# Two engines share the statistics at a stage's end: an interleaved FFT-filter and S4 kernel on one Trainium2 core

## The chip, the cores and the metric

The kernel runs on one core of one Trainium2 chip. The core has four compute engines with a queue of instructions each: TensorE (PE, matrix products; its weight loads are shown apart as PEld), VectorE (DVE), ScalarE (ACT) and GpSimd (POOL). A fifth queue, SyncE (SP), issues most DMA transfers. Each engine works its queue strictly in order, and semaphores hold an instruction until what it needs is done. Matrix products land in PSUM, which the kernel hands out as eight banks of 128 partitions by 512 fp32 numbers; all else is in SBUF. The metric is the device time of one execution in microseconds, the median of several.

## The reference

Two layers, applied in turn and twice (A, B, A, B), on `x` of 2048 positions by 512 channels in fp32:

```python
def _A_ref(x, w_r, w_i):                       # spectral filter (GFNet)
    X = rfft2(x); X = X * (w_r + 1j * w_i)
    return irfft2(X, s=(S, D))
def _B_ref(u, ...):                            # S4 long convolution
    dt = exp(log_dt)[:, None]
    P = exp((dt * A)[:, :, None] * l)          # A = A_re + 1j A_im, l = 0..2047
    K = einsum("dn,dnl,dn->dl", Cc, P, dt * Bc).real
    y = irfft(rfft(pad(u)) * rfft(pad(K)))[:L] # along the positions, 2L long
    return y + u * Dskip
x = x + _A_ref(_layernorm(x), A_w_r, A_w_i)
x = x + _B_ref(_layernorm(x), ...)             # and both once more
```

`_layernorm` takes mean and variance over the 512 channels of a position, with 1e-5 added to the variance. K does not depend on `x`, so its spectrum is computed once.

## The kernel before, in words

**Tiling.** `x` stays in SBUF as 16 "lines" of 128 positions by 512 channels, four to a "group". Both transforms are matrix products with cosine and sine tables, split into factors. Work is cut into pieces, each a small generator that says on which engine its next step runs and what it waits for.

**Stages.** Four stages follow each other: stage 0 (K's spectrum and layer A's first pass, with the norms for layer B), stage 1 (layer B's first pass, called B0 below), stage 2 (layer A's second pass, A2), stage 3 (layer B's second pass, B1). For each, a planner (`Clock`) simulates engines, banks and buffers with fixed costs, and at every moment emits, of the pieces that are ready, the one with the best rank. The ranks are the table `ORDER`: per kind of piece a number for each piece and a shift for each of its steps. What the planner emits is final: it is the order of each engine's queue on the chip, whatever the real times.

**End of A2.** `inv_a(1, s2)` runs once per line: four matmuls L890 into one bank; ScalarE copies it out, L894 and L895; POOL folds it, L901 to L903; one matmul L907; VectorE adds that to the line in three instructions, L911 to L913, and takes its statistics, `moments`, L591 (bn_stats) and L592 (bn_aggr). After each fourth line `spread` has ScalarE take the square root of the group's variances (L625) and VectorE the reciprocal (L627) and the bias −mean × reciprocal (L629). `norm_b` then writes the normed line into `xn`, the upper half of the tile Y, on ScalarE (L639, Identity with a scale and a bias per position).

**Layer B.** `forward_b(r, i)` makes product i of 16: two matmuls (L951; four rows of the profile) into a pair of PSUM banks, over 32 channels of all 16 lines, and therefore after all 16 norms; VectorE transposes the pair into P (L955), which frees the banks. `step_b` makes 16 spectra from these, multiplies them with K's (L963 matmuls, L985 copy of K, L996 on VectorE, L999 and L1003 beside it) and starts the inverse (L1011, copied out by L1018). `turn_b` transposes again (L1034), `inv_b` makes the last matmuls (L1050, L1055), and `close_b` sends the result out. In stage 1 the last pieces of K's spectrum still run at the start: copy L1291, matmul L1309, transpose L1313 and store L1316.

In the working part a row's name tells a tile: `ps` is a PSUM bank, `wk` a working buffer, `x` the lines, `Y` and `Ya` the two large tiles, `mv`, `rs` and `nb` the mean and variance, the reciprocal and the bias of a group.

Of the kernel before, what the change touches and what calls it, by code (L numbers as in the profile page):

```python
# [40 lines left out]
    (0.050611, {"load_in": ([-48.73, -49.67, -13.2, 200.39, 38.48], [21.36, 0]),  # L41
             "load_n": ([170.88], [17.74, 32.32, 39.11, 0]),
             "load_ra": ([122.74], [-34.24, -26.17, 0]),
             "load_h": ([189.13], [-1.1, 0]),
             "load_da": ([87.12], [11.37, 0]),
             "load_rb": ([156.61], [-6.7, 0]),
             "polar_k": ([188.86], [0, 0, -10.23, 4.9, 30.71, 8.86, -8.44, 0]),
             "octant_k": ([195.76], [0, 0, 30.82, 0]),
             "log_k": ([198.17], [7.12, -1.53, 0]),
             "phase_k": ([54.98], [9.47, -22.65, -34.9, -26.84, -10.4, 0]),  # L50
             "parts": ([-1.02, 52.39, 180.27], [-16.65, -3.98, -14.47, -25.06, -3.65, 0]),
             "load_k": ([0.46, 24.35, 26.66, 90.14, 113.68, 14.97, 134.95, 135.35], [-10.85, -5.26, 0]),
             "exp_k": ([31.12, 30.01, 26.72, -30.41, 4.2, 26.79, 11.64, 78.24, -6.3, 0.57, 130.4, 110.04, 7.61, 12.56, -2.93, 102.4, -2.77, 13.49, 75.18, 23.12, 30.66, 48.47, 2.53, 144.61, -3.85, 206.61, 15.72, 29.43, 103.43, 4.73, 22.38, 4.74, 79.71, 78.57, 136.47, 110.99, 104.63, 0.06, 9.23, -3.76, 152.2, 80.58, 107.2, 21.85, 20.82, 98.84, 202.47, 24.5], [-0.87, -2.09, 0]),
             "unit_k": ([-5.49, 9.8, -46.86, 52.48, -7.95, 46.43, 63.91, 65.15, -59.42, -20.7, 96.11, -25.05, -14.14, 82.98, 95.72, 99.58, 47.51, 48.51, 62.41, 78.63, 79.81, 82.78, 85.31, 89.29, 89.73, 95.21, -3.54, 105.55, 118.51, 120.91, 137.32, 137.55], [34.37, 31.83, 13.78, 42.41, 30.07, 30.15, 32.23, 39.12, 35.89, 0]),
             "rows_k": ([48.24, 146.28, 190.46, 133.31, 5.29, 9.15, 119.72, 143.74], [-28.96, -21.87, -21.87, -15.39, -19.71, -19.24, 0]),
             "sums": ([68.3, 174.15, 8.23, 16.19], [32.48, 30.78, 32.04, 16.99, 13.91, 7.66, 34.05, -0.27, 37.66, 2.46, 0]),
             "spread": ([17.55, 129.21, 18.82, 50.21, 18.68, 37.9, 26.12, 42.83, 81.35], [-14.02, -12.43, 0]),
             "moments": ([48.6, 168.25, 167.06, 170.68], [-35.07, 0]),
             "forward_a": ([237.18, 160.57, 32, 190.87, 212.59, 50.71, -0.81, 157.11, 67.95, -12.81, 211.5, 73.12, 9.09, 134.47, 112.18, 101.62], [-41.16, -32.05, -34.91, -48.86, -16.07, 0]),
             "first_a": ([-4.49, -18.8, 15.57, 3.63, 80.21, 17.42, 26.99, 60.31, 117.89, 120.37, 101.06, 141.83, 161.84, 119.48, 213.35, 138.85], [-2.64, 38.82, -12.59, 0.61, 1.12, 22.42, 1.12, 9.82, -0.59, 0.31, 31.16, 0]),  # L60
             "inv_a": ([119.1, 153.39, 154.78, -12.8, 176.52, 180.93, 165.04, 176.64, 179.21, 212.81, 173.77, 172.16, 165.73, 204.44, 203.24, 205.17], [6.59, 5.52, -33.78, -0.86, 39.16, 4.18, 0]),
             "norm_b": ([134.64, -13.39, 180.42, -19.04, 155.44, 123.24, 118.52, -19.66, -9.73, 62, -15.3, 11.32, -33.63, 181.42, 143.72, 95.73], [3.13, 0]),
             "tables": ([52.58], [-16.4, 0])}),
    (0.106371, {"forward_b": ([29.41, 45.28, 85.57, 67.58, 7.03, 50.48, 14.98, 21.28, 109.8, 98.41, 90.83, 85.95, 131.45, 144.47, 19.4, 145.79], [-5.6, -0.98, 0]),
             "step_b": ([7.93, 28.66, 33.01, 13.11, 38.16, 40.28, 33.13, 39.52, 42.94, 57.01, 56.63, 59.65, 66.64, 96.31, 104.01, 83.04], [-17.85, -14.85, -17.85, -16.95, -25.44, -25.72, -28.7, 4.97, -22.24, -44.63, 0]),
             "turn_b": ([44.83, 28.62, 85.03, 95.07, 45.09, 44.66, 52.6, 91.28, 99.52, 44.73, -14.85, 63.29], [3.25, 0]),
             "inv_b": ([119.63, 32.94, 28.08, 78.54, 29.81, 90.22, 22.29, 1.94, 55.77, 84.98, 61.47, 22.25, 20.09, 22.33, 52.81, 56.82], [-14.24, 9.33, 0]),
             "close_b": ([57.52, 57.61, 79.73, 44.41, 4.32, 13.02, 36.04, 99.27], [-0.22, 0]),
             "spread": ([3.27, -6.17, -43.17, -3.6], [44.68, 11.41, 0]),
             "forward_a": ([98.41, 41.14, 22.14, 43, 25.09, 29.39, 49.01, 44.67, 27.43, 43.03, 112.28, 138.34, 59.73, -4.87, 70.46, 89.13], [-11.44, 15.32, -1.65, 0, 11.1, 0])}),  # L70
    (0.010000, {"load_du": ([164.21], [-44.93, 0]),
             "first_a": ([179.48], [-24.75, -4.44, -14.35, 0, 72.12, 2.11, 1.29, 6.33, 6.76, 0.12, 14.34, 0]),
             "group_a": ([194.01, 232.24, 217.79, 202.63, 238.5, 131.16, 205.2, 199.29, 233.37, 217.41, 208.36, 198.07, 122.44, 202.74, 207.67], [-103.75, -39.32, -54.25, -22.22, -23.2, -100.35, -23.93, -3.71, -36.68, -38.02, -25.08, -23.93, 0]),
             "inv_a": ([180.35, 141.51, 145.93, 197.94, 183.36, 101.66, 176.36, 118.03, 147.61, 232.02, 160.93, 213.63, 186.51, 139.07, 199.6, 146.8], [55.08, 1.48, -4.95, -5.13, 25.36, -6.18, -13.95, 0]),
             "spread": ([177.02, 157.89, 140.63, 190.66], [0, -2.36, 0]),
             "norm_b": ([139.04, 206.02, 221.71, 116.37, 218.26, 121.3, 209.11, 190.78, 125.49, 189.55, 217.69, 200.09, 212.22, 217.5, 116.15, 186.47], [-0.59, 0])}),
    (0.191249, {"forward_b": ([16.74, -30.74, 7.86, -14.65, -23.43, -19.05, -24.28, -7.05, 54.87, 33.03, -16.53, 38.87, 21.87, -22.87, 3.42, -24.9], [-14.33, 68.5, 0]),
             "step_b": ([-48.3, -52.59, -66.06, -59.51, -63.91, -44.14, -38.35, -44.74, -47.06, -34.23, -22.73, -28.22, -1.93, -46.76, 16.96, 16.68], [16.57, 35.26, 26.88, 18.48, 44.4, 11.44, 27.32, 94.94, 0]),
             "turn_b": ([-14.27, -34.14, 44.25, 43.22, 23.59, 43.79, -0.43, 14.42, -40.01, 29.56, 38.77, 2.4], [13.89, 0]),
             "inv_b": ([20.94, 61.81, 32.87, 19.49, -33.55, 25.49, 9.2, -18.63, 60.91, -35.33, 1.86, -32.68, 12.23, 21.87, 69.24, 30.39], [76.77, -10.14, 0]),  # L80
             "close_b": ([-46.35, -28.26, 12.32, -60.23, -24.23, 4.46, -64.62, -57.64], [30.99, 0])}),
# [403 lines left out]
class Net:  # L485
# [134 lines left out]
    def spread(self, i, st, act=False, part=slice(0, 4)):  # L620
# [4 lines left out]
        self.nc.scalar.activation(rs, mv[:, :, 1], AF.Sqrt, bias=self.eps)  # L625
        yield "DVE"
        self.nc.vector.reciprocal(rs, rs)  # L627
        if act:
            self.nc.vector.scalar_tensor_tensor(b, mv[:, :, 0], -1.0, rs, op0=OP.mult, op1=OP.mult)  # L629
# [308 lines left out]
    def norm_b(self, r, s2, st):  # L938

        yield "ACT", self.after((id(st), s2)), self.emitted(("group", 1), 16) if r else self.emitted("product", 32)  # L940
        self.norm(s2, st, True, self.xn[r][:, s2, :])
        self.mark("norm_b", r)

    def forward_b(self, r, i):

        nc = self.nc
        yield "PE p:u", self.after(("norm_b", r), 16)
        p = self.psum("u")
        for h in range(2):
# [1 line left out]
            nc.tensor.matmul(p[:, 512 * h:512 * h + 512], self.Rb[o, :], self.xn[r][o, :, 32 * i:32 * i + 32], start=True, stop=True)  # L951
# [561 lines left out]
```

## Time and profile before

| | |
|---|---|
| median of 3 runs | 712.26 us (711.82 to 712.85) |
| profiled execution | 709.7 us, span 707.9 us |
| mean granted TensorE clock | 0.927 |
| PE busy | 580.8 us (82% of the span) |
| DVE busy | 546.8 us (77%) |
| ACT busy | 425.8 us (60%) |
| POOL busy | 314.9 us (44%) |
| share of the chain of waits | PE 12%, DVE 9%, ACT 2% of the span among the largest groups |

The span runs from the first to the last instruction; the execution's time holds 1.8 us more around it. No engine is busy throughout, so the shares say little: what counts is, at each place, which wait ends last. The views that tell this are the chain of waits (what the last instruction waited for, followed back), the busy time by stretches of the span, and the timeline of one engine. In a timeline a row gives start, length, engine, line, operation, tile, and in brackets the idle time before it with what ended it.

### The profile page before, as it was taken

How to read it: one execution, taken by the hardware profiler on the slowest of the kernel's cores; microseconds unless marked ns; L12 is line 12 of the kernel's file. 1: busy time of each engine (PE TensorE's matmuls, PEld its weight loads, DVE VectorE, ACT ScalarE, POOL GpSimd, SP SyncE). 2: the span in 40 equal slices, each digit the busy share in tenths (PEclk: the TensorE clock that was granted, in tenths of full speed). 3: DMA queues.
4: the chain of work that ended last, by engine and by line, in shares of the span. 5: the costliest groups of instructions: out<-in, count | busy, mean ns of one | idle time of the engine just before them, and what ended most of it. 6: DMA issues, size and time to landing. Idle time of an engine off the chain costs nothing. (4 is left out here: it accounts for less than half of the span.)

```text
span 707.9 us, 19921 instructions
## 1 busy us (share of the span) xinstructions
PE 580.8 (82%) x8424; PEld 372.5 (53%) x8424; DVE 546.8 (77%) x807; ACT 425.8 (60%) x742; POOL 314.9 (44%) x299
## 2 busy tenths in 40 slices
PE   0768988989979999796689998579999981789965
PEld 0767866557544444344236564178778750246621
DVE  1697738787697999988694698876988596984994
ACT  6898369898878969787426553067564436035510
POOL 0652108477294462646024562076665670057710
PEclk9969989999999999887699999779999995999996
DMA  8707443221106520101575876260564013025376
GB/s 211 213 16 239 155 130 96 83 74 53 61 25 193 172 75 2 60 4 62 200 274 186 267 243 191 62 262 1 188 228 146 1 44 134 1 92 170 120 213 189
DMA packets 45857, 90.92 MB, mean 128 GB/s; under 512 B 3944, under 2 KB 25960, under 8 KB 44744
## 3 DMA queue, kind: packets, MB, share of 16 engines
q1 hardware_dynamic: 35016, 77.07, 34.4%
q10 hardware_dynamic: 10752, 12.58, 5.0%
q8 instruction: 66, 1.08, 0.6%
q14 instruction: 23, 0.19, 0.1%
HBM read 62.51 MB, written 27.13 MB: 127 GB/s over the span
## 5 line engine op out<-in xcount | busy, mean ns | idle before, releaser
L1003 POOL TENSOR_TENSOR wk<-wk 128x1024 f32<-128x1024 f32 x32 | 75.9, 2380 | 122.7 <-ACT wk L999 122.7
L1269 POOL TENSOR_TENSOR Y<-wk,Y 128x1024 f32<-128x1024 f32 x32 | 76.7, 2396 | 56.2 <-issue 27.6
L1011 PE MATMUL ps<-wk 32*64 32x256 f32 x2048 | 69.7, 381 | 2.5 <-DVE wk L996 0.9
L951 PE MATMUL ps<-Y,cRb 64*128 64x512 f32 x128 | 37.4, 698 | 29.3 <-ACT Y L639 21.7
L1011 PEld LDWEIGHTS ps<-wk 32*64 32x64 f32 x2048 | 47.1, 131 | 26.0 <-issue 7.7
L996 DVE TENSOR_TENSOR wk<-ps,wk 128x1024 f32<-128x1024 f32 x32 | 38.9, 1220 | 24.9 <-PE ps L963 20.3
L1247 DVE SCALAR_TENSOR_TENSOR wk<-wk,ps 128x1024 f32<-128x1024 f32 x32 | 38.9, 1214 | 22.7 <-ACT wk L1245 22.5
L1282 PE MATMUL ps<-Y 128*32 128x64 f32 x2048 | 39.4, 234 | 14.6 <-POOL Y L1270 11.8
L1231 ACT ACTIVATE Y<-ps 128x1024 f32<-128x1024 f32 x48 | 47.7, 1033 | 4.8 <-PE ps L1215 4.5
L1282 PEld LDWEIGHTS ps<-Y 128*32 128x32 f32 x2048 | 34.2, 119 | 29.9 <-POOL Y L1270 21.1
L1215 PE MATMUL ps<-wk,Y 96*128 96x512 bf16 x128 | 40.6, 394 | 8.4 <-ACT Y L1231 4.8
L1050 PE MATMUL ps<-Y,cRbT 128*64 128x512 f32 x128 | 34.5, 692 | 13.9 <-DMA Y<-yi 7.2
L1270 POOL TENSOR_TENSOR Y<-wk,Y 128x512 f32<-128x512 f32 x32 | 43.6, 1363 | 0.0
L999 ACT COPY wk<-ps 128x512 f32<-128x512 f32 x32 | 18.8, 587 | 41.3 <-PE ps L963 35.0
L1263 DVE TENSOR_TENSOR Y<-ps,Y 128x1024 f32<-128x1024 f32 x32 | 38.8, 1213 | 3.2 <-PE ps L1282 2.1
L827 POOL TENSOR_TENSOR x<-x 128x257 f32<-128x257 f32 x16 | 11.6, 723 | 64.4 <-PE ps L850 35.6
L1034 DVE STREAM_TRANSPOSE Y<-Y 128x1024 f32<-128x1024 f32 x16 | 36.7, 2315 | 4.3 <-ACT Y L1018 4.3
L951 PEld LDWEIGHTS ps<-Y,cRb 64*128 64x128 f32 x128 | 12.3, 213 | 52.6 <-ACT Y L639 24.1
L1245 ACT ACTIVATE wk<-ps,magic 128x1024 f32<-128x1024 f32 x32 | 35.5, 1120 | 6.2 <-PE ps L1215 5.9
L1252 ACT ACTIVATE ps<-wk 128x1024 f32<-128x1024 f32 x32 | 32.8, 1026 | 6.3 <-DVE wk L1247 2.4
L1255 ACT ACTIVATE wk<-wk,quarter 128x1024 f32<-128x1024 f32 x32 | 36.4, 1137 | 0.1
L907 PE MATMUL ps<-wk,cRaT 128*128 128x512 f32 x64 | 34.3, 629 | 2.1 <-ACT wk L882 1.9
(232 smaller groups left out, 1631.2 us busy)
## 6 DMA issues: line engine op xcount, KB each, us to landing
yk<-wk SPq DMA_DIRECT2D x8, 1024.0 KB
wk<-yk SPq DMA_DIRECT2D x16, 512.0 KB
khat<-wk ACTq DMA_DIRECT2D x16, 512.0 KB
wk<-khat SPq DMA_DIRECT2D x16, 512.0 KB
Y<-in_W_dram SPq DMA_DIRECT2D x12, 515.0 KB
x<-in_cPa_dram SPq DMA_DIRECT2D x16, 384.0 KB
Y<-in_cGa_dram SPq DMA_DIRECT2D x12, 384.0 KB
x<-in_W_dram SPq DMA_DIRECT2D x16, 258.0 KB
```

What stands on the lines that cost most here:

```text
L951: nc.tensor.matmul(p[:, 512 * h:512 * h + 512], self.Rb[o, :], self.xn[r][o, :, 32 * i:32 * i + 32], start=True, stop=True)
L996: nc.vector.tensor_tensor(t0, X[:, 0, :, None, :].to_broadcast(four), kh[:, 0, None, :, :].to_broadcast(four), op=OP.mult)
L1003: nc.gpsimd.tensor_tensor(t1, xi[:, :, None, :].to_broadcast(four), kh[:, 1, None, :, :].to_broadcast(four), op=OP.mult)
L1011: nc.tensor.matmul(v[i // 2][64 * a:64 * a + 64, 512 * (i % 2):512 * (i % 2) + 256], self.Ib[o, g, a, b, :], t[o, x, k, :], start=n == 0, ...
L1034: self.nc.vector.transpose(y.rearrange("p s d -> p d s"), self.P[r][e][:, :, o:o + 32].rearrange("p k d -> p d k"))
L1215: self.nc.tensor.matmul(p, f[:, c:c + 128], self.oh[:k, o:o + 512], start=True, stop=True)
L1231: nc.scalar.activation(m[:, :, 1024:] if i == 2 else m[:, i, :1024], p.rearrange("p (i m) -> p i m", i=2) if i == 2 else p, AF.Exp)
L1247: nc.vector.scalar_tensor_tensor(s, c, MAGIC, p, op0=OP.subtract, op1=OP.subtract)
L1263: nc.vector.tensor_tensor(E[:, 1, :1024], p, m[:, :1024], op=OP.mult)
L1269: nc.gpsimd.tensor_tensor(E[:, 0, :1024], c, m[:, :1024], op=OP.mult)
L1270: nc.gpsimd.tensor_tensor(rows(E[:, 0, 1024:]), back(c[:, 512:]), rows(m[:, 1024:]), op=OP.mult)
L1282: nc.tensor.matmul(pk[32 * j:32 * j + 32, 64 * e:64 * e + 64], E1[:, r, i, :], E2[:, r, i], start=r == 0, stop=r == 1)
```

## The change

**Statistics on ScalarE.** For groups 0 and 1 of A2's inverse (eight lines, `SQUARED`) `moments` is replaced by two passes of ScalarE over the line: Identity with scale −1/512 and an accumulator, which leaves minus the mean; then Square with that as bias and an accumulator, which leaves 512 times the variance. What the passes write goes into the line's place in `xn`, where the norm overwrites it. The square root of these groups takes the scale 1/512, and the bias's sign is turned.

**Norms on VectorE.** Lines 8 and 9 (group 2) are normed by VectorE (`norm`'s other branch, subtract and multiply) in both passes.

**Products in parts.** Products 4 and 6 of the first pass and 1 and 15 of the second (`FIRST`) are issued in two steps: the columns of groups 0, 1 and 3 when these are normed, and group 2's columns when it is.

**The planner.** ScalarE's passes over SBUF in stages 2 and 3 cost 0.17 more in its own reckoning, and all numbers of `ORDER` are new.

```diff
-    (0.106371, {"forward_b": ([29.41, 45.28, 85.57, 67.58, 7.03, ...
+    (0.105136, {"forward_b": ([7.3, 35.97, 8.14, 55.24, -7.1, ...
...
+SQUARED = 0, 1
+FIRST = (4, 6), (1, 15)
...
+        self.stage = last.stage + 1 if last else 0
...
+                    if self.stage > 1 and n == 512 and ins.opcode == "Activation" and f in ("Identity", "Square") and str(out.space) != str(PSUM):
+                        fixed += 0.17
...
-    def spread(self, i, st, act=False, part=slice(0, 4)):
+    def spread(self, i, st, act=False, part=slice(0, 4), squared=False):
...
-        self.nc.scalar.activation(rs, mv[:, :, 1], AF.Sqrt, bias=self.eps)
+        self.nc.scalar.activation(rs, mv[:, :, 1], AF.Sqrt, bias=self.eps, scale=1.0 / D if squared else 1.0)
         yield "DVE"
         self.nc.vector.reciprocal(rs, rs)
         if act:
-            self.nc.vector.scalar_tensor_tensor(b, mv[:, :, 0], -1.0, rs, op0=OP.mult, op1=OP.mult)
+            self.nc.vector.scalar_tensor_tensor(b, mv[:, :, 0], 1.0 if squared else -1.0, rs, op0=OP.mult, op1=OP.mult)
...
-        yield "DVE"
-        self.moments(s2, st)
+        if r and s2 // 4 in SQUARED:
+            part = self.stat(st, s2 // 4)[:, s2 % 4]
+            yield "ACT"
+            self.nc.scalar.activation(self.xn[r][:, s2, :], xs, AF.Identity, scale=-1.0 / D, accum_out=part[:, 0:1])
+            yield "ACT"
+            self.nc.scalar.activation(self.xn[r][:, s2, :], xs, AF.Square, bias=part[:, 0:1], accum_out=part[:, 1:2])
+            self.mark("moments", id(st), s2)
+        else:
+            yield "DVE"
+            self.moments(s2, st)
...
-        yield "ACT", self.after((id(st), s2)), self.emitted(("group", 1), 16) if r else self.emitted("product", 32)
-        self.norm(s2, st, True, self.xn[r][:, s2, :])
-        self.mark("norm_b", r)
+        act = s2 not in (8, 9)
+        yield "ACT" if act else "DVE", self.after((id(st), s2)), self.emitted(("group", 1), 16) if r else self.emitted("product", 32)
+        self.norm(s2, st, act, self.xn[r][:, s2, :])
+        self.mark("norm_b", r, s2 // 4)
...
-        yield "PE p:u", self.after(("norm_b", r), 16)
-        p = self.psum("u")
-        for h in range(2):
-            o = slice(64 * h, 64 * h + 64)
-            nc.tensor.matmul(p[:, 512 * h:512 * h + 512], self.Rb[o, :], self.xn[r][o, :, 32 * i:32 * i + 32], start=True, stop=True)
+        normed = [self.after(("norm_b", r, k), 4) for k in range(4)]
+        parts = ((0, 8), (12, 16)), ((8, 12),)
+        if i not in FIRST[r]:
+            parts = ((0, 16),),
+        for k, part in enumerate(parts):
+            if k == 0:
+                yield "PE p:u", normed[0], normed[1], normed[3], *normed[2:3] * (len(parts) == 1)
+                p = self.psum("u")
+            else:
+                yield "PE", normed[2]
+            for h in range(2):
+                o = slice(64 * h, 64 * h + 64)
+                for a, b in part:
+                    nc.tensor.matmul(p[:, 512 * h + 32 * a:512 * h + 32 * b], self.Rb[o, :], self.xn[r][o, a:b, 32 * i:32 * i + 32], start=True, stop=True)
...
-                yield self.spread(s2 // 4, sa, True)
+                yield self.spread(s2 // 4, sa, True, squared=s2 // 4 in SQUARED)
```

The lines move with the change: of those named above L894 and L895 become L899 and L900, L907 becomes L912, L911 to L913 become L916 to L918, L591 and L592 become L596 and L597, L625, L627 and L629 become L630, L632 and L634, L639 becomes L644 (and VectorE's norm is L646), L951 becomes L974, L955 becomes L978, L963 becomes L986, L996 becomes L1019, L1011 becomes L1034, L1313 becomes L1336. L923 and L925 are the two new passes.

What the new numbers do to the queues is told by the order in which each engine's instructions are issued. First ScalarE at the end of A2; before, after the last copies of the inverse, it ran:

```order
L894 COPY wk<-ps 128x384
L895 COPY wk<-ps 128x128
L625 ACTIVATE rs<-mv,eps 128x4
L639 ACTIVATE Y<-x,nb,rs 128x512 x4
L625 ACTIVATE rs<-mv,eps 128x4 x2
L639 ACTIVATE Y<-x,nb,rs 128x512 x8
L625 ACTIVATE rs<-mv,eps 128x4
L639 ACTIVATE Y<-x,nb,rs 128x512 x4
```

It now runs, from the last two lines' copies on:

```order
L899 COPY wk<-ps 128x384
L900 COPY wk<-ps 128x128
L644 ACTIVATE Y<-x,nb,rs 128x512 x4
L925 ACTIVATE Y,mv<-x,mv 128x512
L923 ACTIVATE Y,mv<-x 128x512
L630 ACTIVATE rs<-mv,eps 128x4
L925 ACTIVATE Y,mv<-x,mv 128x512
L630 ACTIVATE rs<-mv,eps 128x4
L644 ACTIVATE Y<-x,nb,rs 128x512 x8
L630 ACTIVATE rs<-mv,eps 128x4
L644 ACTIVATE Y<-x,nb,rs 128x512 x2
```

The first of the eight pairs of passes starts after the copy of the sixth line; from there a copy and one or two passes alternate, and the last two lines' passes stand behind four norms. The queue ends with two norms in place of four.

VectorE at the same place; before, the last two lines' adds and their statistics come right ahead of the first transpose:

```order
L911 TENSOR_TENSOR x<-x,ps 128x512
L912 TENSOR_TENSOR x<-x,ps 128x256
L913 TENSOR_TENSOR x<-x,ps 128x256
L591 BN_STATS st<-x 128x6
L592 BN_AGGR mv<-st 128x2
L591 BN_STATS st<-x 128x6
L592 BN_AGGR mv<-st 128x2
L627 RECIPROCAL rs<-rs 128x4
L629 SCALAR_TENSOR_TENSOR nb<-mv,rs 128x4
L955 STREAM_TRANSPOSE Y<-ps 128x32x32
```

And now, from a reciprocal that waits for ScalarE:

```order
L632 RECIPROCAL rs<-rs 128x4
L634 SCALAR_TENSOR_TENSOR nb<-mv,rs 128x4
L916 TENSOR_TENSOR x<-x,ps 128x512
L917 TENSOR_TENSOR x<-x,ps 128x256
L918 TENSOR_TENSOR x<-x,ps 128x256
L596 BN_STATS st<-x 128x6
L597 BN_AGGR mv<-st 128x2
...
L632 RECIPROCAL rs<-rs 128x4
L634 SCALAR_TENSOR_TENSOR nb<-mv,rs 128x4
L646 TENSOR_SCALAR Y<-x,mv,rs 128x512 x2
L978 STREAM_TRANSPOSE Y<-ps 128x32x32
```

Three lines' statistics end the adds there, and the two norms of group 2 come between the last reciprocal and the first transpose.

Last, TensorE early in B0; before, two products stood in the place of the spectra's last pieces and the first inverse matmul came soon after:

```order
L951 MATMUL ps<-Y,cRb 128x512 x2
L963 MATMUL ps<-wk 32x256 x16
L951 MATMUL ps<-Y,cRb 128x512 x2
L1011 MATMUL ps<-wk 64x256 x32
L963 MATMUL ps<-wk 32x256 x16
L963 MATMUL ps<-Y,wk 32x256 x16
L1011 MATMUL ps<-wk 64x256 x32
```

And now:

```order
L974 MATMUL ps<-Y,cRb 128x512 x2
L986 MATMUL ps<-wk 32x256 x16
L974 MATMUL ps<-Y,cRb 128x512 x8
L1034 MATMUL ps<-wk 64x256 x32
L986 MATMUL ps<-wk 32x256 x16
L986 MATMUL ps<-Y,wk 32x256 x16
L1034 MATMUL ps<-wk 64x256 x32
```

Four products, eight matmuls, stand ahead of the first L1034 where one stood; the three come from further back in the same queue.

More of the change, by code (lines that the diff above doesn't have):

```diff
@@ L40 @@
 ORDER = [
[L41 to L81, printed above, removed]
+    (0.050611, {"load_in": ([2.14, -31.49, 60.38, 195.95, 62.39], [-5.34, 0]),
+             "load_n": ([162.77], [21.6, 34.91, 21.6, 0]),
+             "load_ra": ([111.95], [-8.08, -14.65, 0]),
+             "load_h": ([138.52], [-14.4, 0]),
+             "load_da": ([122.57], [-9.59, 0]),
+             "load_rb": ([118.83], [-21.66, 0]),
+             "polar_k": ([180.49], [0, -15.92, -10.39, 4.9, 6.15, 0.23, -15.07, 0]),
+             "octant_k": ([-12.75], [18.15, 17.08, 71.2, 0]),
+             "log_k": ([125.26], [13.96, -7.38, 0]),
+             "phase_k": ([82.15], [-18.39, -50.67, -60.78, -68.43, -44.46, 0]),
+             "parts": ([96.23, 121.16, 171.19], [29.55, 16.72, 5.01, -3.36, -47.62, 0]),
+             "load_k": ([5.09, 26.52, 38.33, 89.4, 129.67, 134.53, 17.57, 178.23], [4.96, 1.73, 0]),
+             "exp_k": ([30.04, 4.85, 39.82, 0.5, 7.05, 21.91, 8.12, 114.54, 9.72, -11.15, 158.96, -1.55, 22.25, 18.32, -65.23, 8.09, -12.99, 16.82, 18.92, 20.05, -19.18, 49.28, -12.85, 150.98, 3.52, 17.05, 115.34, -8.23, -2.37, 199.57, 32.51, 1.41, 34.85, 76.23, 129.16, 113.74, 97.49, 112.01, -1.27, 8.21, -12.83, 140.78, 133.71, -13.21, 125.47, 105.46, -1.42, -33.61], [-1.6, -0.73, 0]),
+             "unit_k": ([-7.31, 10.27, -40.19, 49.73, -12.86, -6.94, 66.86, 70.18, -99.11, -8.78, 103.47, -30.03, -33.82, 76.29, 84.35, 110.62, 41.65, 57.36, 64.29, 81.46, 79.97, 85.01, 87.58, 87.74, 88.39, 91.69, 61.12, 94.43, 102.28, 114.56, 128.37, 134.44], [37.07, 32.4, 26.45, 46.25, 33.05, 33.13, 35.21, 42.1, 38.01, 0]),
+             "rows_k": ([38.49, 144.37, 196.76, 142.7, -45.1, 2.59, 38.57, -12.82], [-30.33, -13.55, -27.23, -15.5, -23.48, -11.99, 0]),
+             "sums": ([116.72, 84.23, 27.49, 23.58], [5.29, 23.25, 2.88, -1.55, 4.82, 5.29, 11.65, 5.29, 27.57, -19.83, 0]),
+             "spread": ([4.69, 75.48, -22.97, 94.08, 11.95, 71.94, -24.27, 113.82, -3.16], [11, 8.59, 0]),
+             "moments": ([162.83, 151.37, 116.25, 133.96], [-22.25, 0]),
+             "forward_a": ([193.6, 186.31, 16.84, 148.27, 107.84, 111.78, -0.37, 9.05, 83.39, -5.4, 107.22, 116.39, -17.2, 125.87, 145.17, 70.04], [-12.92, 0, -2.69, 0.82, 15.59, 0]),
+             "first_a": ([-15.91, -11.05, 8.37, -2.97, 87.71, 10.51, 22.14, 56.52, 105.03, 131.34, 99.53, 134.5, 157.68, 122.1, 202.53, 125.71], [26.37, 43.51, -2.16, 10.99, 11.14, 44.66, 17.33, 22.39, 9.43, 10.42, 34.93, 0]),
+             "inv_a": ([158.52, 158.55, 184.82, 25.76, 196.79, 223.38, 200.56, 217.82, 215.08, 255.07, 213.57, 196.11, 216.97, 239.72, 239.02, 246.73], [-20.37, -20.71, -60.82, -27.92, -0.75, -20.44, 0]),
+             "norm_b": ([-23.5, -12.28, 191.19, 71.08, -21.33, 152.29, 126.27, 107.8, -18.26, -14.58, -25.67, 169.56, -6.26, 160.12, -32.74, -12.32], [16.65, 0]),
+             "tables": ([185.33], [-3.26, 0])}),
@@ new lines @@
+    (0.105136, {"forward_b": ([7.3, 35.97, 8.14, 55.24, -7.1, 73.99, -3.89, 11.45, 102.42, 103.84, 84.86, 41.36, 78.66, 130.53, 89.7, 155.34], [0, 0, 0, 0]),
+             "step_b": ([-17.39, 8.44, 9.05, -9.19, 15.93, 17.95, 15.79, 17.6, 23.17, 36.24, 38.6, 38.72, 40.43, 71.23, 87.32, 34.43], [0, 3.05, -9.43, 0, -29.6, -39.25, -6.78, 22.83, -3.22, -22.29, 0]),
+             "turn_b": ([99.34, 57.11, 28.87, 50.3, 98.06, 52.47, 34.24, 40.65, 32.08, 32.79, 58.7, 35.78], [-6.98, 0]),
+             "inv_b": ([115.97, 29.37, 50.03, 108.39, 26.8, 83.27, 59.31, 39.77, 43.81, 31.98, 46.92, 42.04, 22.86, 17.23, 43.11, 98.77], [-9.4, -1.97, 0]),
+             "close_b": ([30.12, 35.45, 15.32, -4.31, -14.94, -2.88, 8.18, 86.38], [13.97, 0]),
+             "spread": ([-14.16, 1.48, 16.98, 4.38], [37.31, -17.11, 0]),
+             "forward_a": ([81.45, 19.05, 9.45, 34.8, 23.87, 15.41, 29.61, 33.95, 19.46, 32.56, 112.68, 126.35, 45.67, -13.62, 72.85, 81.44], [0.82, 14.3, 0.76, -12.25, 22.66, 0])}),
@@ new lines @@
+    (0.031999, {"load_du": ([194.57], [-15.79, 0]),
+             "first_a": ([205.02], [-1.2, -12.06, 13.75, 14.65, -16.88, -1.2, -23.83, 25.44, -1.2, 29.72, 21.52, 0]),
+             "group_a": ([212.99, 172.94, 104.05, 215.53, 212.52, 214.19, 214.56, 216.33, 209.11, 207.36, 219.67, 291.66, 234.52, 211.79, 287.99], [-95.65, 21.93, -16.17, -8.61, -11.99, -84.46, -19.04, -13.08, -6.8, -14.76, -11.99, -10.72, 0]),
+             "inv_a": ([188.54, 193.2, 189.01, 183.83, 182.56, 225.2, 175.76, 213.72, 239.14, 253.12, 161.25, 249.52, 220.51, 187.97, 196.46, 181.4], [26.52, 6.79, 27.31, 26.52, 31.05, 18.53, 35.39, 34.29, 0]),
+             "spread": ([211.25, 229.65, 206.65, 209.67], [28.41, 27.23, 0]),
+             "norm_b": ([210.53, 215.64, 169.47, 208.06, 243.73, 212.06, 215.16, 237.54, 198.67, 207.63, 223.83, 260.36, 187.99, 215.98, 207.14, 183.48], [20.92, 0])}),
@@ new lines @@
+    (0.179424, {"forward_b": ([-49.41, -65.14, -17.17, -24.21, 13.92, -40.69, -40.24, -22, -28.55, -19.35, -40.46, 16.18, 17.75, 39.95, -57.29, 5.42], [5.51, 0, 20.64, 0]),
+             "step_b": ([-60.8, -53.04, -36.98, -36.9, -63.31, -30.31, -40.43, -29.24, -21.04, -65.95, -17.13, -16.28, -27.43, -11.82, 31.72, 15.04], [-46, 2.47, -12.53, -24.15, -20.34, -4.17, 20.57, 79.5, 0]),
+             "turn_b": ([47.07, -39.46, -18.53, 7.53, -14.87, -49, -50.75, 30.41, 33.8, 43.38, -21.58, -72.5], [11.69, 0]),
+             "inv_b": ([-57.63, 17.06, -55.02, 20.83, 4.36, -69.09, -58.55, -56.44, -80.43, -41.11, -30.64, 27.3, -36.24, -65.44, -73.88, 30.5], [101.41, -0.1, 0]),
+             "close_b": ([-52.47, 3.4, 37.92, 10.23, -37.61, -74.4, -19.79, -41.15], [22.98, 0])}),
```

## The prediction, on record before the result was known

> **What bounds the kernel now.** I read the chain of waits first, around the place where layer A's second pass hands over to layer B's. Its columns are start, length and work.
>
> ```profile
> 553.10 3.84 PE ps L890 x32
> 556.94 0.90 PE ps L907 x2
> 557.86 0.70 DVE x L911
> ...
> 589.91 4.17 ACT Y L639 x6
> ...
> 594.93 0.20 ACT rs L625
> ...
> 595.57 2.94 ACT Y L639 x4
> 598.54 2.13 PE ps L951 x4
> 600.69 1.94 DVE Y L955
> ```
>
> TensorE starts the inverse, then VectorE takes the chain at 557.86 and keeps it, add after add and statistic after statistic, until ScalarE gets the last eight norms. The first product of layer B starts only at 598.54, because it reads columns of all sixteen normed lines. The table by stage says the same.
>
> ```profile
> 553.00:582.00 29.00, 28.58 (x160) 20.23 (x160) 23.35 (x56) 10.42 (x33) 24.98 (x61) 1.00 0.01 2
> 582.00:599.00 17.00, 0.46 (x2) 0.46 (x4) 11.81 (x34) 12.64 (x20) 0.00 (x0) 0.55 0.47 182
> 590.00:594.00 4.00, 0.00 (x0) 0.00 (x0) 3.86 (x10) 4.00 (x7) 0.00 (x0) 0.50 0.08 33
> 598.00:602.00 4.00, 3.46 (x8) 1.52 (x10) 1.31 (x1) 0.49 (x1) 0.00 (x0) 0.50 0.00 0
> 602.00:606.00 4.00, 4.00 (x16) 1.75 (x14) 4.00 (x4) 0.00 (x0) 0.00 (x0) 0.74 0.00 0
> ```
>
> The columns are the stretch, its length, busy time of PE, PEld, DVE, ACT and POOL, the granted clock, the DMA share and GB/s. PE is full to 582 and then does 0.46 us in 17. ScalarE did only 10.42 of the 29 us before that: there is room, but only while PE is the pace. When PE comes back, its clock is 0.50.
>
> **Part 1: statistics to ScalarE (end of A2).** The VectorE timeline prices what leaves it.
>
> ```profile
> 561.56 0.68 DVE L911 TENSOR_TENSOR x<-x,ps 128x512 f32<-128x512 f32 x1
> 562.94 0.69 DVE L591 BATCH_NORM_STATS2 st<-x 128x6 f32<-128x512 f32 x1
> 563.76 0.66 DVE L591 BATCH_NORM_STATS2 st<-x 128x6 f32<-128x512 f32 x1
> ...
> 593.84 0.18 DVE L592 BATCH_NORM_AGGREGATE mv<-st 128x2 f32<-128x6 f32 x1
> ```
>
> A line's three adds take 562.94 − 561.56 = 1.38 us, its statistics 563.76 − 562.94 = 0.82. Eight lines lose their statistics: 8 × 0.82 = 6.6 us off a queue that ended at 594.0. PE and ScalarE show the pace at which lines come.
>
> ```profile
> 575.18 1.05 PE L890 MATMUL ps<-wk,Ya 128*128 128x128 f32 x8
> 576.93 1.05 PE L890 MATMUL ps<-wk,Ya 128*128 128x128 f32 x8
> 562.33 0.48 ACT L894 COPY wk<-ps 128x384 f32<-128x384 f32 x1 [1.10 <-PE ps L890]
> 562.71 0.27 ACT L895 COPY wk<-ps 128x128 f32<-128x128 f32 x1
> 564.08 0.48 ACT L894 COPY wk<-ps 128x384 f32<-128x384 f32 x1 [1.10 <-PE ps L890]
> ```
>
> PE takes 1.75 us a line, and ScalarE idles 1.10 of each. The forms that go there do not occur in this stage; the nearest rows are stage 0's passes with an accumulator, on lines of the same size.
>
> ```profile
> 9.50 0.61 ACT L607 ACTIVATE Y<-x 128x512 f32<-128x512 f32 x1
> 10.02 0.19 ACT L607 ACTIVATION_READ_ACCUMULATOR Y<-x 128x1 f32 x1
> 10.11 0.70 ACT L609 ACTIVATE Y<-x,sa 128x512 f32<-128x512 f32 x1
> 10.72 0.19 ACT L609 ACTIVATION_READ_ACCUMULATOR Y<-x,sa 128x1 f32 x1
> 10.81 0.61 ACT L607 ACTIVATE Y<-x 128x512 f32<-128x512 f32 x1
> ```
>
> From start to start they cost 0.61 and 0.70 us, the accumulator reads lying inside. Pass plus copies is 1.31 + 0.65 = 1.96 for a line whose statistics moved, against 1.75 on PE, so ScalarE falls behind slowly and is what ends last. I walk its new queue from the copy of the seventh line (562.33; one first pass has been issued): 10 copies × 0.65 = 6.5; 8 second passes × 0.70 = 5.6; 7 first passes × 0.61 = 4.3; 3 square roots × 0.2 = 0.6; 12 norms at the pitch of this row,
>
> ```profile
> 583.75 2.93 ACT L639 ACTIVATE Y<-x,nb,rs 128x512 f32<-128x512 f32 x4 [1.34 <-DVE nb L629]
> ```
>
> 2.93/4 = 0.73 each, 8.8. That is 25.8 us; the gaps in which it still waits for PE's next line come to about 2.1 when its times are laid beside PE's 1.75. So groups 0, 1 and 3 are normed at 562.33 + 25.8 + 2.1 = 590.2. VectorE's queue meanwhile has two waits more: the reciprocal for group 3 stands behind a square root that ScalarE gives at about 583.4, with the adds of lines 14 and 15 and three statistics after it, and ends at about 589.3, so it is not last. Group 2's square root, reciprocal and bias end at 590.8, and its last two ScalarE norms at 592.3. VectorE's two norms have no row; the nearest is a scale-and-shift of the same tile,
>
> ```profile
> 44.03 0.42 DVE L1090 TENSOR_SCALAR Y<-Y 128x512 f32<-128x512 f32 x1
> ```
>
> 0.42 each, done by 591.7 beside ScalarE's. If they took 0.73 as ScalarE's do, they would end at 592.3, still not late.
>
> [...]
>
> **Part 2: first products in parts.** Two of the sixteen products take their columns of groups 0, 1 and 3 first: three quarters of 2.13 us each at the half clock, 2 × 1.6 = 3.2, from 590.2 to 593.4. Group 2's quarter of the first follows: 0.53, to 594.0. The first transpose then starts at 594.0 instead of 600.69: **−6.7 us**. The bounds: −8.0, when ScalarE waits for nothing extra and the clock is up earlier; −3.7, when the accumulator reads do not hide (8 × (0.19 + 0.19) = 3.0 us).
>
> [...]
>
> What follows keeps its order on every engine, and no load is late: the DMA share is 0.08 from 590 to 594. PE and the stores run behind this start to the end, so the gain passes whole.
>
> **Part 3: layer B's first pass (B0).** Here two norms also go to VectorE, and three of sixteen products are emitted ahead of the first inverse matmuls.
>
> ```profile
> 335.03 0.35 ACT L1291 COPY wk<-ps 128x256 f32<-128x256 f32 x1
> 335.39 1.28 ACT L625 ACT_TABLE_LOAD   x1
> 341.31 1.91 DVE L1313 STREAM_TRANSPOSE wk<-ps 128x1024 f32<-128x1024 f32 x1
> 341.49 2.93 ACT L639 ACTIVATE Y<-x,nb,rs 128x512 f32<-128x512 f32 x4 [0.79 <-DVE nb L629]
> 344.47 7.19 PE L951 MATMUL ps<-Y,cRb 64*128 64x512 f32 x24 [4.93 <-ACT Y L639]
> 346.67 3.67 DVE L955 STREAM_TRANSPOSE Y<-ps 128x1024 f32<-128x1024 f32 x2 [3.45 <-PE ps L951]
> 366.57 5.71 DVE L955 STREAM_TRANSPOSE Ya<-ps 128x1024 f32<-128x1024 f32 x3
> 367.29 1.13 PE L951 MATMUL ps<-Y,cRb 64*128 64x512 f32 x4
> 368.62 1.75 PE L1011 MATMUL ps<-wk 32*64 32x256 f32 x53 [0.21 <-DVE Ya L955]
> 380.00:400.00 20.00, 19.73 (x552) 11.68 (x533) 11.15 (x8) 11.22 (x17) 9.46 (x4) 1.00 0.68 222
> ```
>
> Two norms fewer on ScalarE would be 1.5 us, but its last kernel copy (335.03) now stands behind the table load and a norm, 1.28 + 0.35 or 1.65 later, and the transposes of K behind it (the last, 341.31 to 343.2, now ends near 345.0) hold VectorE's second norm until 345.5. The first transpose starts at 346.1 instead of 346.67: −0.55. Then the products: a product needs a pair of PSUM banks that a transpose has left, and the transposes run at 5.71/3 or less, 1.75 to 1.90 each. Three more ahead of the first L1011 put that from 368.62 to about 373.7: +5.1. PE has meanwhile done three products (1.07 each) that it had to do later: −3.2. From 380 PE is full (19.73 of 20), so what is lost stays: +1.9. Bounds 0 (the inverse had slack) and −1 to +5.3 (all six transposes must end first). Net **+1.35**.
>
> **Part 4: the other renumbered orders.** In stage 0 some matmuls of K's factors and ScalarE copies change places with neighbours, with as many table loads; the rest keeps its order. 0, bounds ±1.
>
> **The sum** is −6.7 − 0.55 + 1.9 = −5.35: span 707.9 to 702.55, the profiled execution 709.7 to 704.35. The median of the runs is 2.56 above that execution, so 712.26 − 5.35 = **706.9 us**.
>
> **The rivals.**
>
> *A smaller loss in B0.* PE has work to pull forward and the three products cost nothing: −6.7 to −8 with at most +0.5, about **704.5**. For: spectra of K are ready from the same loads. Against: PE's 0.21 us wait at 368.62 is on such a transpose.
>
> *The gain shrinks.* The accumulator reads and the reciprocals that wait for ScalarE's square roots cost: −3.7 + 1.35 = −2.35, **709.9**, and about 711 if B0's loss goes towards its bound. For: three reciprocals now sit in VectorE's queue ahead of adds whose PSUM tiles PE needs. Against: stage 0's start to start of 0.61 and 0.70.
>
> *ScalarE paces the inverse (slower).* Its queue is in order, and each line's copy stands behind a pass that needs the adds of an earlier line. If passes run end to end with their reads, 0.61 + 0.19 + 0.70 + 0.19 = 1.69, with the copies' 0.48 + 0.27 a line takes 2.44 against PE's 1.75: ten lines late by 0.69, +6.9, which eats part 2's 6.7, and B0 adds 1.35: about +1.6, **713.9**. It decides from a cadence of 2.4 us a line. For: PE's wait would spread to POOL and VectorE, which have no other work. Against: the pitches of stage 0 are measured on the same engine and size. [...]
>
> *That nothing is done early.* If the parts' products wait for all sixteen norms, the end is 592.3 + 2.1 = 594.4 for the first transpose: 0.4 worse, inside the forecast.
>
> **How the numbers follow.** Forecast 0.58 (705 to 709), smaller loss 0.13, shrunk gain 0.18, slower 0.11. About 0.2%, 1.4 us, is what a measurement of this kernel can tell from no change. Faster: 0.58 + 0.13 + 0.10 of the shrunk gain = 0.81; the same: its other 0.08; slower 0.11. The range, 703.5 to 711.2, leaves out the slower case and the tips of two others.
>
> **What would show it.** In the changed profile: ScalarE's passes at 0.61 and 0.70 from start to start, the copies' cadence below 2 us a line, groups 0, 1, 3 normed near 590, the first transpose of B1 near 594 less what B0 lost, and the first inverse matmul of B0 near 373.7. A cadence above 2.4, or a start of B0's PE-full stretch more than 5 us late, makes the prediction wrong; so does any shift before 330 by more than 1 us.

## The result

The kernel became slower: 721.88 us median (719.41 to 722.59, 6 runs) against 711.15 (707.75 to 712.85, 6 runs) beside it, a ratio of 1.0151, 95% interval 1.0122 to 1.0179. The profiled execution's span is 720.6 us against 707.9, 12.7 us more. The forecast was 706.9 us, with a range of 703.5 to 711.2. The medians differ by 10.7 us; the two profiled executions, 709.7 and 722.5 us, lie a little apart from them in opposite directions, so some 2 us of the 12.7 below are the spread between executions.

Milestones tell where the 12.7 us arose. Each is the start of the first row of its kind in a timeline, in us from the span's start.

| | before | changed | later by |
|---|---|---|---|
| first product of B0 (TensorE) | 344.47 | 357.30 | 12.8 |
| first transpose of B0 (VectorE) | 346.67 | 360.80 | 14.1 |
| first inverse matmul of B0 | 368.62 | 386.17 | 17.6 |
| start of A2's inverse | 553.10 | 573.29 | 20.2 |
| first transpose of B1 | 600.69 | 613.43 | 12.7 |
| end of the span | 707.9 | 720.6 | 12.7 |

Stage 0 lost 12.8 us, B0 up to A2's inverse 7.4 more, the end of A2 won 7.5, and B1 neither won nor lost. The rows of the changed kernel's TensorE behind three of these, and one ahead of them:

```profile
244.44 1.03 PE L1238 MATMUL ps<-wk,Y 96*128 96x512 bf16 x2 [9.40 <-DMA Y<-spe]
...
357.30 6.61 PE L974 MATMUL ps<-Y,cRb 64*128 64x256 f32 x36 [3.90 <-DVE wk L1336]
...
386.17 0.66 PE L1034 MATMUL ps<-wk 32*64 32x256 f32 x8 [0.59 <-DVE Ya L978]
...
609.94 6.58 PE L974 MATMUL ps<-Y,cRb 64*128 64x256 f32 x36 [8.01 <-ACT Y L644]
```

The last row is the place of the 16.79 us wait before: it is 8.01 now. The first is new. TensorE waits 9.40 us for a load, `Y<-spe`, and in the kernel before no row of that stretch has such a wait. Summed over the line, what ended TensorE's idle time, before and now:

```profile
  DMA Y<-spe: 4.8, 2
```

```profile
  DMA Y<-spe: 24.2, 4
```

(The sum counts a wait of the weight load and of its matmul each.) `spe` holds the factors of K's exponentials in DRAM; `load_k` fetches them in eight blocks, and the matmuls of block b need block b's load. SyncE's queue, before and then changed (the loads between the first two rows are left out):

```profile
89.20 0.75 SPq L1206 DMA_DIRECT2D Y<-spe  x1
...
201.79 0.76 SPq L1206 DMA_DIRECT2D Y<-spe  x1
...
211.42 27.12 SPq L559 DMA_DIRECT2D x<-in_A_x_dram  x32
238.65 0.79 SPq L1206 DMA_DIRECT2D Y<-spe  x1
```

```profile
90.82 0.75 SPq L1229 DMA_DIRECT2D Y<-spe  x1
...
202.75 0.76 SPq L1229 DMA_DIRECT2D Y<-spe  x1
...
212.38 27.51 SPq L564 DMA_DIRECT2D x<-in_A_x_dram  x32
239.99 0.79 SPq L1229 DMA_DIRECT2D Y<-spe  x1
```

The rows read alike. Six blocks are loaded ahead of 32 loads of x, which hold the queue for 27 us, and the last two behind them. But the name does not say which block. The two numbers in `ORDER` do: `load_k`'s ranks for blocks 5 and 6 were 14.97 and 134.95, and are 134.53 and 17.57. In the written lists of the next section the blocks stand, with the old ranks, in the order 0, 5, 1, 2, 3, 4, then x, then 6 and 7, so that block 5 came at 89.20 and block 6 at 238.65. With the new ranks it is 0, 6, 1, 2, 3, 4, then x, then 5 and 7: block 6 comes at 90.82 and block 5 at 239.99, behind x. TensorE still takes block 5 first. It waits from 235.04 on; the load is issued 4.9 us later and TensorE goes on another 4.5 us later, 9.4 us in all.

The end of A2 went as forecast. ScalarE there:

```profile
587.24 0.63 ACT L923 ACTIVATE Y<-x 128x512 f32<-128x512 f32 x1
587.76 0.20 ACT L923 ACTIVATION_READ_ACCUMULATOR Y<-x 128x1 f32 x1
587.85 0.47 ACT L899 COPY wk<-ps 128x384 f32<-128x384 f32 x1
588.21 0.28 ACT L900 COPY wk<-ps 128x128 f32<-128x128 f32 x1
588.37 0.74 ACT L925 ACTIVATE Y<-x,mv 128x512 f32<-128x512 f32 x1
588.99 0.21 ACT L925 ACTIVATION_READ_ACCUMULATOR Y<-x,mv 128x1 f32 x1
589.49 0.48 ACT L899 COPY wk<-ps 128x384 f32<-128x384 f32 x1 [0.29 <-PE ps L895]
```

A first pass takes 0.61 us from its start to the next instruction's, with the accumulator read inside; a pair of copies 0.52 to 0.56 rather than 0.65. At most of the lines ScalarE still waits for TensorE (0.29 us in the last row), and the matmuls L895 keep their 1.75 us a line, so the copies do not slow the inverse.

### The profile page after: what moved, and what is told of

Same layout as the page of the kernel before. It is cut to its first block, busy times and chain, and to the rows that moved or that the text cites. A ratio compares the mean times of both kernels' runs of the same rounds, so it can differ in the third digit from the quotient of the medians.

```text
span 720.6 us, 19994 instructions
## 1 busy us (share of the span) xinstructions
PE 583.9 (81%) x8456; PEld 377.1 (52%) x8456; DVE 544.1 (76%) x795; ACT 433.2 (60%) x770; POOL 314.8 (44%) x299
## 5 line engine op out<-in xcount | busy, mean ns | idle before, releaser
L1034 PE MATMUL ps<-wk 32*64 32x256 f32 x2048 | 71.5, 388 | 4.7 <-DVE Ya L978 2.3
L1019 DVE TENSOR_TENSOR wk<-ps,wk 128x1024 f32<-128x1024 f32 x32 | 39.2, 1228 | 31.8 <-PE ps L986 31.7
L1034 PEld LDWEIGHTS ps<-wk 32*64 32x64 f32 x2048 | 47.9, 133 | 28.6 <-issue 6.5
L1238 PE MATMUL ps<-wk,Y 96*128 96x512 bf16 x128 | 42.5, 419 | 18.1 <-DMA Y<-spe 11.7
L974 PE MATMUL ps<-Y,cRb 64*128 64x512 f32 (+2 forms) x160 | 37.4, 587 | 21.9 <-ACT Y L644 8.0
L1057 DVE STREAM_TRANSPOSE Y<-Y 128x1024 f32<-128x1024 f32 x16 | 37.1, 2336 | 4.3 <-ACT Y L1041 4.3
L974 PEld LDWEIGHTS ps<-Y,cRb 64*128 64x128 f32 x160 | 15.9, 224 | 42.5 <-DVE Y L978 18.0
L1332 PE MATMUL ps<-wk,cRk 32*128 32x512 f32 x128 | 32.5, 674 | 5.3 <-ACT wk L1314 4.3
```

Of the source, the lines that this page charges most:

```text
L974: nc.tensor.matmul(p[:, 512 * h + 32 * a:512 * h + 32 * b], self.Rb[o, :], self.xn[r][o, a:b, 32 * i:32 * i + 32], start=True, stop=True)
L1019: nc.vector.tensor_tensor(t0, X[:, 0, :, None, :].to_broadcast(four), kh[:, 0, None, :, :].to_broadcast(four), op=OP.mult)
L1034: nc.tensor.matmul(v[i // 2][64 * a:64 * a + 64, 512 * (i % 2):512 * (i % 2) + 256], self.Ib[o, g, a, b, :], t[o, x, k, :], start=n == 0, ...
L1057: self.nc.vector.transpose(y.rearrange("p s d -> p d s"), self.P[r][e][:, :, o:o + 32].rearrange("p k d -> p d k"))
L1238: self.nc.tensor.matmul(p, f[:, c:c + 128], self.oh[:k, o:o + 512], start=True, stop=True)
```

## The experiments

Except for the exchange in the kernel before, the planner's choice was replaced by a written list of pieces, so that only what is named moves:

```diff
-            t, p = min((e for e in ready if e[0] <= self.now + near), key=lambda e: e[1][:2])
+            name = seq.pop(0)
+            p = next(p for p in pieces if p[6] == name)
```

**The load of block 5, in both kernels.** In the kernel before, two ranks are exchanged, and in the profiles every engine keeps the order of its lines; in the changed kernel, two entries of its own list are exchanged back.

```diff
-             "load_k": ([0.46, 24.35, 26.66, 90.14, 113.68, 14.97, 134.95, 135.35], [-10.85, -5.26, 0]),
+             "load_k": ([0.46, 24.35, 26.66, 90.14, 113.68, 134.95, 14.97, 135.35], [-10.85, -5.26, 0]),
```

```diff
-422: load_k:6    834: load_k:5
+422: load_k:5    834: load_k:6
```

> The kernel before with one exchange in the order: the loads of K's factor blocks 5 and 6 change places on SyncE's queue, so that block 5's stands behind the 32 loads of x. Nothing else moves. Theory A (this exchange is what the change lost in its first stage): TensorE waits some 9.4 us near 235 us for block 5's load, the first layer-B product comes 9 to 13 us late, time 720.5 to 724 us against 711.2. Theory B (the loss came from the other exchanged pieces of stage 0, the wait is only where it showed): within 1.4 us of the kernel before.

> The changed kernel, its order written out, with the loads of blocks 5 and 6 exchanged back; no other instruction moves. Theory A: the changed kernel less 9.4 to 12.8 us, 709 to 712.5 us, and the first layer-B product back to 344.5 to 348 us. Theory B: 721 to 722 us, as the changed kernel.

Measured: the kernel before with the exchange 721.47 us (ratio 1.0159, 1.0116 to 1.0202), the first product of B0 at 357.64 instead of 344.47, and this row:

```profile
245.56 1.04 PE L1215 MATMUL ps<-wk,Y 96*128 96x512 bf16 x2 [9.71 <-DMA Y<-spe]
```

From the first product on, its milestones keep the distances of the kernel before (209.2 us to A2's inverse against 208.6; 47.6 from there to B1's first transpose in both). The changed kernel without the exchange: 712.55 us (1.0026, 0.9997 to 1.0054), first product at 347.25, 10.0 us earlier than in the changed kernel. So two loads that change places make the whole difference between slower and not slower. This is shown in both directions.

**The second half alone.** The kernel before, with the end of A2 as changed:

```diff
-        act = s2 not in (8, 9)
+        act = not r or s2 not in (8, 9)
...
-FIRST = (4, 6), (1, 15)
+FIRST = (), (1, 15)
```

with stages 0 and 1 in the old order, 2 and 3 in the new.

> The kernel before with the change's second half alone: statistics of eight lines on ScalarE, two norms on VectorE and two products in parts in the second pass, and the new order of stages 2 and 3; stages 0 and 1 in the old order, with the old norms and whole products. Theory A (the second half gains what the traces show, 20.2 us of delay before the inverse becoming 12.7 at the first transpose): 7.5 us less than before, 703.7 us. Theory C (that gain was only time that a late start had given to loads): 708 us or more.

Measured: 703.57 us, ratio 0.9908 (0.9874 to 0.9941). From the inverse's start to B1's first transpose 40.24 us, against 47.59 before and 40.14 in the changed kernel: 7.4 us, whether or not the kernel comes there late. Theory C falls.

**What of the second half carries it.** Three kernels, each the one above with one part undone: statistics on VectorE, whole products, norms on ScalarE.

```diff
-SQUARED = 0, 1
+SQUARED = ()
```

```diff
-FIRST = (), (1, 15)
+FIRST = (), ()
```

```diff
-        act = not r or s2 not in (8, 9)
+        act = True
```

> As the kernel with the second half alone (703.6 us), with all sixteen lines' statistics on VectorE again; the norms on VectorE, the parts and the order stay. Measured from the inverse's start to the first transpose of the second layer-B pass: 47.6 us before, 40.2 with the whole second half. Theory A (the statistics carry it): 8 x 0.82 us come back to VectorE's queue, less what its queue waited; 45.5 to 47 us, 709 to 711 us in time. Theory B (the norms and parts carry it): 41 to 43 us, 704.5 to 706.5.

> As the kernel with the second half alone, with products 1 and 15 of the second pass issued whole, after all sixteen norms. From the inverse's start to the first transpose: theory A (the parts hide most of the last group's wait) 40.2 plus 0.8 to 1.2 us, since a whole product at the half clock takes 2.1 us from the last norm; theory B (nothing, since the products are bound elsewhere) 40.2.

> As the kernel with the second half alone, with the norms of lines 8 and 9 of the second pass on ScalarE, behind the two that it has there. From the inverse's start to the first transpose: theory A 40.2 plus 1.4 us (two norms of 0.73 more at the end of ScalarE's queue, the last quarter of the first product behind them); theory B (the two engines share the write into the same lines and gain nothing) 40.2 plus less than 0.5.

> The kernel before with the second half alone and whole products, once more with more rounds: theory A (the parts give nothing at the end, the first transpose they bring forward is lost among the transposes behind it) 702 to 704 us, the same as with the parts (703.6); theory B (the parts cost something behind the first transpose) below 702.

| | inverse's start to first transpose | time, ratio to before |
|---|---|---|
| before | 47.59 | |
| second half | 40.24 | 703.57, 0.9908 (0.9874 to 0.9941) |
| without statistics on ScalarE | 44.47 | 706.90, 0.9958 (0.9932 to 0.9985) |
| without parts | 40.94 | 701.96, 0.9882 (0.9804 to 0.9960) |
| the same again | 40.93 | 701.79, 0.9880 (0.9853 to 0.9908) |
| without norms on VectorE | 41.07 | 703.25, 0.9895 (0.9860 to 0.9930) |

The statistics are worth 4.2 us, which lies between what the two theories expected. In the kernel without them VectorE's queue ends like this:

```profile
594.45 0.66 DVE L764 BATCH_NORM_STATS2 st<-x 128x6 f32<-128x512 f32 x1
595.14 0.18 DVE L765 BATCH_NORM_AGGREGATE mv<-st 128x2 f32<-128x6 f32 x1
595.86 0.18 DVE L800 RECIPROCAL rs<-rs 128x4 f32<-128x4 f32 x1 [0.54 <-ACT rs L798]
596.08 0.16 DVE L802 SCALAR_TENSOR_TENSOR nb<-mv,rs 128x4 f32<-128x4 f32 x1
596.16 1.00 DVE L814 TENSOR_SCALAR Y<-x,mv,rs 128x512 f32<-128x512 f32 x2
599.08 1.91 DVE L1146 STREAM_TRANSPOSE Y<-ps 128x1024 f32<-128x1024 f32 x1 [1.92 <-PE ps L1142]
```

It is full to 595.3, 40.7 us after the inverse's start (554.61); before, it was full to 594.0, 40.9 after 553.10. So VectorE is the bound again, and most of what is still won comes behind it, in the norms and the parts. These are worth 0.8 and 0.7 us at that place. The three parts of the edit undone singly cost 4.2, 0.7 and 0.8, 5.8 together, of the 7.4: the rest is shared between them or lies in the new order, which no run separates. For the parts and for the norms the measured place lies between what the two theories expected (0.7 against 0.8 to 1.2 or nothing, 0.8 against 1.4 or below 0.5). In the time neither can be told: the kernels without parts and the one without norms on VectorE are not slower, and 701.79 us for the repeat does not decide between 702 and below. The kernel without parts is the fastest found, 701.8 us; it beats both kernels, and its interval overlaps that of the second half with parts.

**B0: the old order, three products, the parts.** First the changed kernel with the loads exchanged back and stage 1 in the old order with whole products; the two norms stay on VectorE.

> As the changed kernel with the loads exchanged back, and stage 1 (layer B's first pass) in the order of the kernel before, its products whole; the two norms of that pass stay on VectorE. Theory A (three products ahead of the first inverse matmuls cost layer B's first pass 4 to 6 us, as the traces show between its first transpose and the next inverse): 4 to 6 us less than the changed kernel with the loads exchanged back, 704 to 708 us. Theory D (the later loss there comes from the late start or from the norms): the same within 1.5 us as that kernel.

Measured: 706.34 us, ratio 0.9933 (0.9906 to 0.9960), and 208.02 us from the first product to A2's inverse (before 208.63; 216.47 with the loads exchanged back alone). So B0's loss of 7.8 us is in its order and parts, not in the norms or the late start. Then the same kernel with the new stage 1, in which only products 9, 13 and 15 go back behind the first inverse matmuls; and that one with products 4 and 6 whole.

> The changed kernel with the loads of blocks 5 and 6 exchanged back, and with only three of layer B's first-pass products (9, 13 and 15, with their transposes) moved back behind the first inverse matmuls, to the places that the kernel before gives its last three. Measured by the time from the first product of that pass to the next stage's inverse: 208.6 us before, 216.5 with the loads exchanged back alone. Theory A (the three products are the cost): 208.5 to 210.5, and 6 to 8 us less in time than with the loads exchanged back alone. Theory B (the prediction's sum: 5.1 late less 3.2 done early): about 214.6, 1.9 us less. Theory C (the cost comes from the rest of the order, or from the products in parts): 216, no difference.

> As the kernel with the loads exchanged back and three products moved back, with products 4 and 6 of the first pass whole again. From that pass's first product to the next inverse: 211.1 us with the parts, 208.6 before. Theory A (both parts stand ahead of the first whole product, and the first transpose comes 3.5 us after the first matmul instead of 2.2): 209.5 to 210. Theory B (the rest of the order costs the remaining 2.5): 211.

| | first product to first transpose | from there to the first inverse matmul | from there to A2's inverse | sum |
|---|---|---|---|---|
| before | 2.20 | 21.95 | 184.48 | 208.63 |
| loads exchanged back | 3.53 | 25.38 | 187.56 | 216.47 |
| three products back too | 3.48 | 21.97 | 185.63 | 211.08 |
| and whole products | 2.11 | 22.00 | 183.66 | 207.77 |

Times 707.52 us (0.9961, 0.9929 to 0.9993) and 705.23 (0.9929, 0.9894 to 0.9964). The three products cost 5.4 us of the 7.8 (by the ratios of the times 0.65%, 4.6 us): 3.4 up to the first inverse matmul and 1.9 more behind it. The sum of 211.08 just misses the 208.5 to 210.5 that theory A expected. The 1.9 is less firm than the 3.4: the third column is 187.1 and 187.6 in the two kernels with the products ahead, and 181.8 to 185.0 in the eight with the old order of stage 1. The 2.0 us there between the last two rows are no more than that spread. The parts cost 1.4 at the front, because two first parts stand ahead of the first product's last quarter while hardly anything is gained. The rows of VectorE, with the loads exchanged back:

```profile
345.23 1.88 DVE L1506 STREAM_TRANSPOSE wk<-ps 128x1024 f32<-128x1024 f32 x1
346.98 0.46 DVE L816 TENSOR_SCALAR Y<-x,mv,rs 128x512 f32<-128x512 f32 x1
350.78 10.59 DVE L1148 STREAM_TRANSPOSE Y<-ps 128x1024 f32<-128x1024 f32 x6 [3.35 <-PE ps L1144]
```

The first part starts at 347.25, after the transpose of K that ends at 347.11 and leaves a pair of banks. The last norm ends at 347.44. So the parts run only 0.2 us ahead of the norm that they are meant to hide. That is theory A's mechanism; its sum of 209.5 to 210 was still above the 207.77 measured. What happens at the first inverse matmuls is seen on TensorE, with the three products ahead and then back:

```profile
372.70 2.87 PE L1144 MATMUL ps<-Y,cRb 64*128 64x512 f32 x12 [0.22 <-DVE Ya L1148]
376.16 0.66 PE L1204 MATMUL ps<-wk 32*64 32x256 f32 x8 [0.59 <-DVE Ya L1148]
377.89 3.64 PE L1204 MATMUL ps<-wk 32*64 32x256 f32 x56 [1.07 <-DVE Ya L1148]
381.46 1.09 PE L1156 MATMUL ps<-wk 64*32 64x256 f32 x32
```

```profile
373.70 1.99 PE L1204 MATMUL ps<-wk 32*64 32x256 f32 x64 [0.22 <-DVE Ya L1148]
375.62 1.09 PE L1156 MATMUL ps<-wk 64*32 64x256 f32 x32
```

The same 64 matmuls take from 376.16 to 381.46, 5.3 us, instead of 1.9. TensorE waits for transposes, 0.59 and 1.07 us, and its clock is down:

```profile
372.00:376.00 4.00, 3.35 (x16) 0.99 (x12) 4.00 (x4) 0.54 (x1) 2.04 (x1) 1.00 0.84 262
376.00:380.00 4.00, 2.77 (x48) 1.68 (x56) 4.00 (x4) 0.00 (x0) 0.00 (x0) 0.74 0.02 8
380.00:384.00 4.00, 4.00 (x112) 2.23 (x104) 1.76 (x2) 2.19 (x3) 0.00 (x0) 0.83 0.15 18
```

The granted clock is 0.74 and 0.83, where the kernel with the three products back has 1.00 throughout.

**What is left of stage 0.** In the four kernels that have the changed stage 0 with its loads exchanged back, the first product of B0 starts at 347.25 to 348.60; in the six with the old stage 0, at 344.47 to 347.09. The means differ by 2.3 us. A copy shows where some of it is. ScalarE in the one of these kernels that has the old stage 1, and TensorE there:

```profile
337.65 1.28 ACT L800 ACT_TABLE_LOAD   x1
338.95 0.30 ACT L800 ACTIVATE rs<-mv,eps 128x4 f32<-128x4 f32 x1
339.15 0.80 ACT L814 ACTIVATE Y<-x,nb,rs 128x512 f32<-128x512 f32 x1
339.86 0.35 ACT L1484 COPY wk<-ps 128x256 f32<-128x256 f32 x1
```

```profile
348.60 7.00 PE L1144 MATMUL ps<-Y,cRb 64*128 64x512 f32 x24 [4.23 <-DVE Y L816]
```

K's last copy comes 2.2 us after the table load starts, with the matmuls, the transposes of K and VectorE's second norm in a row behind it, and the first product waits for that norm. The copy stood ahead of the table load before. That this is all of the 2.3 us was not tried.

## Why the prediction was wrong

**The step that failed is part 4**, "The other renumbered orders": "some matmuls of K's factors and ScalarE copies change places with neighbours, with as many table loads; the rest keeps its order. 0, bounds ±1." The order lists the loads by tile and size, and two loads of two blocks have the same row, so a list in which they change places reads as unchanged. Measured at the first product of B0, the exchange costs 10.0 us in the changed kernel and 13.2 in the one before (12.0 against the mean of the six kernels with its stage 0); by the ratios of the times it is about 9 and 11. Another 2.8 us of stage 0 (2.3 between the means) are in the rest of its new order, against the same term of 0. The prediction had named the sign itself, a shift before 330 by more than 1 us; it came at 244. Where the moved instructions have the same name, the row that counts is that of the wait (which load a matmul needs first), or the table of ranks itself.

**Part 1 and part 2 held in their sum.** Forecast −6.7 (−8.0 to −3.7), measured −7.4. The passes came at 0.61 and about 0.72 us, as in stage 0, with the reads hidden. TensorE's cadence stayed 1.75 (590.10 to 591.85), and with groups 0, 1 and 3 normed the first part started 36.65 us after the inverse (forecast 590.2 − 553.1 = 37.1). VectorE's norms took 1.00 for two, where the nearest row gave 0.84. The in-order rival, ScalarE at 2.4 us a line, did not happen: the copies' cadence in the changed kernel is 1.75 in the mean of nine lines, from 582.51 to 598.25. For these eight lines ScalarE's passes are the dearer ones, 1.33 us a line against 0.82, and the place is still 4.2 us shorter. But the sum gave the gain to the statistics and the parts; the runs give 4.2 to the statistics, 0.8 to the norms, to which the sum gave nothing, and 0.7 to the parts, which does not show in the time; 1.6 are not assigned.

**The clock was taken as half throughout, at little cost.** The 0.74 of the kernel before, over 602 to 606, is 0.50 to about 604.1 and 1.00 behind it: the half clock lasts 5.5 us from the first product. In the changed kernel it lasts 3.3 us, and over the twelve profiles 3.0 to 7.9 us at this place. In four kernels the clock stays at 0.50 until the first transpose, which comes 3.55 to 3.56 us after the first part; in three it is back just before, and that takes 3.38 to 3.49. So the sum's 3.7 was 0.2 too long even at the half clock throughout, and the clock is worth another 0.1 to 0.2.

**Part 3 failed too, in its return and in its start.** The three products were put at +5.1 late and −3.2 for work done early, +1.9 in all. Measured is +5.4. They put the first inverse matmul 3.4 late; then 64 matmuls take 3.4 more, with waits and at the lower clock, for which the sum had no term. Some 1.1 us are returned up to the first turn on VectorE and 0.3 behind it, not 3.2; why not more stays open. The start was put at −0.55 by letting the first transpose follow the last norm by 0.6 (345.5 to 346.1), as if the first parts were done by then. With the loads exchanged back it follows by 3.3 (347.44 to 350.78), since the first parts wait for banks; whole products are 1.4 faster there. The last norm itself ends 1.9 later than forecast, in the rest of stage 0's order.

So of 12.7 us, 10 are the loads, 2.8 the rest of stage 0, 7.4 B0, and −7.5 the end of A2. The slower rival had the right sign with a mechanism that played no part, and the chance of 0.11 for slower left no room for a queue that had been read as unchanged.

## What to carry to other kernels

When a planner's numbers change, compare the identity of what is moved, not the rows' names: for each load, which block it carries, what stands ahead of it on its queue, and which instruction needs it first. A load that slips behind a long burst costs, on the engine that needs it, what is left of the burst and its own way (here 4.9 and 4.5 us), and that can be more than the edit was meant to gain. Keep each stage's order apart when trying a change: here the new orders of the last two stages, with the edits there, were worth 1%, those of the first two were not worth taking, and the sum hid the gain.
